# GpSimd's weight sums in other slots, resident blocks filled later, queries loaded in the second layers: a linear-attention and GELU kernel on one core

## The chip, the core and the metric

The kernel runs on one core of one Trainium2 chip. TensorE (PE) multiplies, VectorE (DVE), ScalarE (ACT) and GpSimd (POOL) work on tiles in SBUF and in PSUM, and SyncE (SP) issues the DMAs, one after the other from one queue. The metric is the time of one execution in microseconds (us) of device time; of several runs the median counts. Beside the runs there is one profiled execution with its trace.

## The reference

Linear attention, an RMS norm per head, and a feed-forward network with a GELU, all in fp32:

```python
kv  = einsum('bhsd,bhse->bhde', k, v)            # b=8, h=8, s=576, d=64
o   = einsum('bhsd,bhde->bhse', q, kv)
o   = o / sqrt(mean(o*o, axis=-1) + 1e-6) * g_norm
x   = o.transpose(0, 2, 1, 3).reshape(4608, 512)
h   = x @ w_in                                   # 512 x 2048
y   = (0.5 * h * (1 + erf(h / sqrt(2)))) @ w_out # 2048 x 512
```

## The kernel before

**Arithmetic.** Each operand of the two layers is split into a high part that TensorE's fp32r format holds exactly and a low part, the rest. A product is then three matmuls: high by high, high by low, low by high. The low parts are subtractions on VectorE: `low_x` (L351) and `low_block` (L376) for x, `rest` (L708) for the activations, `low_sums` (L454) and the second half of `split_out` (L1050) for sums of weights. The high parts are copies on ScalarE (`split_out`'s is L1049).

**Chunks.** The 4608 tokens are nine chunks of 512. In chunks 0 and 1 both layers are plain: a chunk has 16 *slots*, and slot i computes one 128-wide block of h (`layer1`, L689, 12 matmuls of 512 columns), its GELU on ScalarE, and what the block before adds to the output (`layer2`, L716, 12 matmuls of 512 columns). Chunk 2 has a plain second layer, but its first layer goes in eight *pairs* of blocks, each by a product form of the Winograd kind with seven products of half size in place of eight (`layer1_pair`, `product` at L554, 12 or 6 matmuls of 256 columns each; L570 copies the first product out of PSUM and L545 adds the rest). In chunks 3 to 8 both layers have this form: the first layer goes in parts (`first_part`, `second_part`, numbered j = 0 to 7, the second part of j following the first part of j + 1), the second layer in 28 *ticks* of 12 matmuls of 256 columns (L1247). `FAST` is 3, `PLAIN` is 2, `NCH` is 9.

**Sums of weights.** The seven-product form wants sums of weight blocks. Those of w_in are made on VectorE in chunk 1 (`sum_weights`: whole blocks at L427, half sums at L438, low parts at L454; `HALVES` tells how many in which slot). Those of w_out are made in eight groups j = 0 to 7: `sum_out(j)` on GpSimd puts together two whole blocks (two additions of 128x512) and makes four sums of 128x256 (all L545); `split_out(j)` then makes the high and low parts, and `send` issues the DMAs that put the products into DRAM. Group 0 is made in slots 12 and 13 of chunk 0, group 1 from slot 15 of chunk 0, groups 2, 3 and 4 in slots 4, 6 and 13 of chunk 1, groups 5, 6 and 7 in pairs of chunk 2. The first addition of each `sum_out` waits for the last GELU that was issued ahead of it, by a dependence written by hand, so that it doesn't start sooner.

**Fetches.** The products of weights lie in DRAM as blocks of 512 KB. `fetch` (L505) brings them into a ring of six SBUF slots, in the order of their use; `used` issues the next fetch as soon as a slot's last reader is issued. Nine blocks of the second layer and some of the first stay resident in SBUF. The pieces of the resident blocks that need no sum are copied from the weights in SBUF by `raw_out(j)` through `product_out` (L411, a DMA from SBUF to SBUF, three of 256 KB for each j).

**Other transfers.** The same SP queue carries the queries of the next chunk but one (`Attn.load`, L222, two loads of 512 KB for a chunk), K and V (`load_kv` L151 and L168, `load_main` L123, `load_tails` L138) and the output (L755 to L758). In the fast chunks the attention of chunk c + 1 is computed during chunk c: its projection and squares in the first layer (`within_layer1`; the fold of the squares is L293), its operands for the first layer in the second (`within_layer2`).

Tile names: `w_in_…`, `w_out_…`, `x_…` and `s_…` are places in SBUF that are reused for many things; only the number behind the name tells one use from the next. `products_in_…` and `products_out_…` are the blocks in DRAM.

Of the kernel before, what the change touches and what calls it, by code (L numbers as in the profile page):

```python
# [8 lines left out]
F32 = mybir.dt.float32  # L9
# [3 lines left out]
ALU = mybir.AluOpType  # L13
# [10 lines left out]
FAST = 3  # L24
# [13 lines left out]
def linear_attn_rms_gelu_ffn(  # L38
# [24 lines left out]
    NF = w_in.shape[0]  # L63
    NCH = NT // CH
# [33 lines left out]
    SPARE = ["s0", "s1", "s2"]  # L98
# [9 lines left out]
        block_tile(name, F32)  # L108


    kv_in, late = {}, {}

    def late_tile(name):

# [88 lines left out]
    class Attn:  # L203
# [144 lines left out]

        def low_x(self, p, eng):
            hi, lo = (self.x[p][:, z].rearrange("p (a n) -> p a n", a=2) for z in range(2))  # L350
            eng.tensor_tensor(out=lo, in0=self.pair(p), in1=hi.bitcast(F32), op=ALU.subtract)  # L351

        def add_blocks(self, k, eng=nc.vector):
            to, a, op, b = {
# [30 lines left out]
    NJ2 = NF // 2  # L385
# [144 lines left out]
    free = []  # L530
# [230 lines left out]
    attn = [Attn(c) for c in range(NCH)]  # L761
    first, second = attn[:2]
# [44 lines left out]
    for d in range(0, 2 * D, BLK):  # L807
        h = d // D * D
        nc.gpsimd.tensor_tensor(
            out=fold[:, d:d + BLK], in0=ident[:, h:h + BLK], in1=ident[:, h + BLK:h + 2 * BLK],  # L810
# [181 lines left out]
    def raw_out(j):  # L992

        t = [parts["out", 2 * j + n].rearrange("p (a n) -> p a n", a=2) for n in range(2)]
        product_out(place_out(j, 0), t[0][:, :, :HALF])
        product_out(place_out(j, 4), t[1][:, :, :HALF])
        product_out(place_out(j, 3), t[1][:, :, HALF:])
# [8 lines left out]
    RAW = [x for j in range(4) for x in ((raw_in, j + 1), (raw_out, j))]  # L1006
    RAW += [(raw_in, 0), (raw_out, 4), (raw_in, 5), (raw_out, 5), (raw_in, 6), (raw_in, 7)]

    wide, sent, latest = {}, [], {}

    def sum_out(j, places=()):

        eng = nc.gpsimd
        if places:
            name = of = None
            whole, s = (block_tile(n, F32)[:, :2 * DM] for n in places)
        else:
            (name, whole), (of, s) = take(), take()
        for n in range(2):
            w = parts["out", 2 * j + n].bitcast(F32)  # L1020
            op = add(whole[:, n * DM:(n + 1) * DM], w[:, HI], w[:, LO], eng=eng)
            if n == 0:
                tc.add_manual_dep(
                    op.ins, latest["gelu"].ins.name,
                    mybir.DependencyInfo(
                        mybir.DependencyClass.Sync, mybir.DependencyReason.DATA
                    ),
                )
        a11, a21, a12, a22 = (whole[:, n * HALF:(n + 1) * HALF] for n in range(4))
        s1, s2, s3, s4 = (s[:, n * HALF:(n + 1) * HALF] for n in range(4))  # L1030
        for o, x, op, y in (
            (s1, a21, ALU.add, a22), (s2, s1, ALU.subtract, a11),
            (s3, a11, ALU.subtract, a21), (s4, a12, ALU.subtract, s2),
        ):
            add(o, x, y, op, eng)
        if name:
            free.append(name)
        wide[j] = of, s
# [41 lines left out]
        for n in {9: (0, 1), 14: (2, 3), 15: (4, 5)}.get(i, ()):  # L1080
            fetch(n)

    EARLY = (0, 0, 4, 6, 13)
    SQUARES = (2, 3, 5, 6)
    HALVES = {1: 2, 2: 2, 3: 2, 4: 1, 5: 1, 7: 2, 8: 1, 9: 1, 10: 1, 11: 2, 12: 1}
    order = list(range(3, len(weights)))

    last = [2]
# [32 lines left out]
    for s in range(PLAIN * NF):  # L1121
        c, i = divmod(s, NF)
        h[s] = layer1(attn[c], i)
        if i == 1 and c:
            store(acc.pop(c - 1), (c - 1) * CH, both=False)
        if c and i in (1, 4):
            place_kv(c + 1, (0, 1) if i == 1 else (2, 3))
        if c == 0:
            g[s] = gelu(h.pop(s))
            if s == 1:  # L1130
                sum_kv(1, (2, 3), kv_ps[1, 0])

            def between():
                if i == 0:
                    for p in (2, 3):
                        attn[0].low_x(p, nc.vector)
                if i in (9, 10):
                    high_w(i - 9)
                    low_w(i - 9)
                if i == 10:  # L1140
                    load_w(len(weights) - 1)
                if i == 1:
                    place_kv(1, range(NP))
                spread_work(c, i)

            convert(i, lambda: g.update({s: rest(*g[s])}), between)
            if s:
                second_layer(s - 1)
            spread_matmuls(c, i)
            if i in (7, 8):  # L1150
                load_kv(c + 2, i - 7)
            if i == 8:
                attn[c + 2].load(0)
            for _ in range(2):
                if i > 6 and RAW:
                    store_raw, j = RAW.pop(0)
                    store_raw(j)
            if i == 12:
                sum_out(0, SPARE[:2])
            if i == 13:  # L1160
                split_out(0, (SPARE[2], SPARE[0]))
                send()
            if i == 15:
                sum_out(1, (SPARE[1], SPARE[0]))
        else:
            spread_matmuls(c, i)
            g[s] = gelu(h.pop(s))
            nxt, k = attn[c + 1], SQUARES.index(i) if i in SQUARES else None
            if k is not None:
                sq = nxt.square(BLOCKS[k])  # L1170
            if i == 12:
                for p in (2, 3):
                    load_kv(c + 2, p)
            sum_weights(i, HALVES.get(i, 0), lambda: g.update({s: rest(*g[s])}))
            if k is not None:
                nxt.reduce(BLOCKS[k], sq)
            if i and i in EARLY:
                sum_out(EARLY.index(i), ("w_in9", SPARE[0]) if i == 13 else ("w_in2", "w_in3"))
            elif i - 1 in EARLY:
                n = max(1, EARLY.index(i - 1))  # L1180
                split_out(n, (SPARE[2:0:-1], ("w_in4", "w_in5"), ("w_in6", "w_in7"),
                              SPARE[1:])[n - 1])
            spread_work(c, i)
            second_layer(s - 1)
            later(c, i)
# [155 lines left out]
    def within_layer1(c, j, second):  # L1341


        nxt = attn[c + 1] if c + 1 < NCH else None
        aft = attn[c + 2] if c + 2 < NCH else None
        at = j, second
        if nxt:
            if second and j < 2 and c == FAST:
                nxt.project(j, [bank(f"a{half}") for half in range(2)])
                for half in range(2):  # L1350
                    nxt.squares((j, half))
            if not second and j < 2 and c > FAST:
                if j == 0:
                    for k, name in enumerate(("acc2", "acc3", "a0", "a1")):
                        nxt.ps[k // 2, k % 2] = bank(name)
                    for p in range(NP):
                        nxt.project_pair(p)
                for half in range(2):
                    nxt.squares((j, half))
            if at == (2, True):  # L1360
                nxt.inv = nxt.rsqrt(nxt.fold(bank("a0")))
            if at in SCALES:
                nxt.scale(SCALES.index(at), nc.gpsimd)
            for k in {(6, False): ("T3", "T1"), (5, True): ("T2", "T4")}.get(at, ()):
                nxt.add_blocks(k, nc.gpsimd)
        if second and c + 2 < B:
            late = int(c == FAST)
            if j - late in (2, 3):
                names["kv", j - late], t = take()
                load_main(c + 2, j - late, t)  # L1370
            if j - late == 3:
                load_tails(c + 2)
            if j - late == 5:
                kv_ps[c + 2, 0] = bank("a1")
                sum_kv(c + 2, range(NP), kv_ps[c + 2, 0])
                free.extend(names.pop(n) for n in (("kv", 2), ("kv", 3), "tails"))
                place_kv(c + 2, range(NP))
        if second and aft and j in (1, 2):
            aft.load(j - 1)

    def next_piece(c, n, eng):
        nxt = attn[c + 1]
        name, t = take(F32R)
# [3 lines left out]

    def within_layer2(c, layer, i):

        if c + 3 < B and i in (8, 18):  # L1390
            load_kv(c + 3, i // 18)
        if c + 1 < NCH:
            step = len(layer.ticks) // 8
            if i % step == step - 1 and i // step < NPR:
                n = i // step
                next_piece(c, n, nc.vector)

    free += ["x4", "x5", "x0", "x1", "w_in12"] + SPARE
    SUMS = {1: (5,), 3: (6,), 5: (7,)}
    SPLITS = {2: (5,), 6: (6,), 7: (7,)}  # L1400
    STEPS = ((3, 1), (3, 2), (4, 0), (4, 2))
    for c in range(PLAIN, FAST):
        for j in range(NJ2):
# [31 lines left out]
    for c in range(FAST, NCH):  # L1435
# [3 lines left out]
        for j, second in parts_of_layer1():  # L1439
# [7 lines left out]
                    send()  # L1447
            else:
                second_part(at, j, blocks)
            if c == FAST and second and j in (2, 5):  # L1450
                raw_out(NJ2 - 2 + j // 3)
                free.extend(f"w_out{n + 2 * (j // 3)}" for n in (NF - 4, NF - 3))
            if j < NJ2 - 1:
                within_layer1(c, j, second)
            if (j, second) == (NJ2 - 1, False):
# [70 lines left out]
```

## Time and profile before

| | before |
|---|---|
| median of 3 runs (lowest to highest) | 787.66 us (785.92 to 788.44) |
| the profiled execution's own time | 787.64 us |
| its span from the first to the last instruction | 785.8 us |
| PE busy | 777.2 us (99%), 6460 matmuls |
| DVE, ACT, POOL busy | 573.6, 352.1, 163.5 us |
| DMA | 239.10 MB, mean 304 GB/s; SP's queue takes 84.8% of 16 engines' span |
| granted TensorE clock | 1.000 of full speed |

Busy time is what an engine spends in instructions; PE's ends are modelled. A row of the list of waits names the engine and tile that waited, what released it, the total in us, the count and the longest. A row of the chain or the timeline gives a start in us from the span's beginning, a duration, an engine, a line and an operation; the timeline also gives the tile written and those read, how many instructions it took together, and in square brackets the idle time before it with what ended it.

### The profile page before, as it was taken

How to read it: one execution, taken by the hardware profiler on the slowest of the kernel's cores; microseconds unless marked ns; L12 is line 12 of the kernel's file. 1: busy time of each engine (PE TensorE's matmuls, PEld its weight loads, DVE VectorE, ACT ScalarE, POOL GpSimd, SP SyncE). 2: the span in 40 equal slices, each digit the busy share in tenths (PEclk: the TensorE clock that was granted, in tenths of full speed). 3: DMA queues.
4: the chain of work that ended last, by engine and by line, in shares of the span. 5: the costliest groups of instructions: out<-in, count | busy, mean ns of one | idle time of the engine just before them, and what ended most of it. 6: DMA issues, size and time to landing. Idle time of an engine off the chain costs nothing.

```text
span 785.8 us, 16444 instructions
## 1 busy us (share of the span) xinstructions
PE 777.2 (99%) x6460; PEld 726.7 (92%) x6460; DVE 573.6 (73%) x1035; ACT 352.1 (45%) x667; POOL 163.5 (21%) x142
## 2 busy tenths in 40 slices
PE   9999999999999999999999999999999999999998
PEld 7888878888899989899999999999999999999998
DVE  3998886798657773769477947795689668965783
ACT  3777545434452332437243624362536343632461
POOL 1000160421223210450027001800171017101200
PEclk9999999999999999999999999999999999999999
DMA  9997966666796789997999798979997989799974
GB/s 347 407 396 255 332 208 241 208 233 241 282 360 220 259 268 370 362 375 284 351 355 362 273 366 319 381 256 319 312 364 257 319 305 323 256 316 340 334 250 168
DMA packets 88368, 239.10 MB, mean 304 GB/s; under 512 B 8804, under 2 KB 29796, under 8 KB 88292
## 3 DMA queue, kind: packets, MB, share of 16 engines
q1 hardware_dynamic: 88288, 238.06, 84.8%
q8 instruction: 51, 0.84, 0.4%
q14 instruction: 25, 0.20, 0.1%
q10 hardware_dynamic: 4, 0.00, 0.0%
HBM read 199.23 MB, written 34.08 MB: 297 GB/s over the span
## 4 chain that ended last, share of the span: by engine, by line
PE 93%; DMA 3%; DVE 2%; issue 1%; ACT 0%; SPq 0%; DVEq 0%; ACTq 0%
PE acc L1247 21%; PE acc L554 18%; PE acc L716 16%; PE h L554 15%; PE h L689 10%; PE a L1247 8%; PE a L188 2%; PE a L241 1%; DMA kv_main<-kv_main 1%; DMA w_in<-products_in 1%; DMA w_in<-qT 1%; PE acc L241 1%; PE h L679 0%; DVE x L351 0%; DVE x L376 0%
## 5 line engine op out<-in xcount | busy, mean ns | idle before, releaser
L716 PE MATMUL acc<-w_out,gh 128*128 128x512 f32 x312 | 97.1, 392 | 0.0
L689 PE MATMUL h<-x,w_in 128*128 128x512 f32 x360 | 87.4, 391 | 0.6 <-DVE x L351 0.6
L689 PEld LDWEIGHTS h<-x,w_in 128*128 128x128 f32 x360 | 67.3, 188 | 15.6 <-DVE x L351 1.3
L716 PEld LDWEIGHTS acc<-w_out,gh 128*128 128x128 f32 x312 | 57.7, 188 | 12.2 <-ACT s L1049 0.2
L702 ACT ACTIVATE gh<-h 128x512 fp32r<-128x512 f32 x39 | 23.3, 597 | 92.5 <-PE h L689 62.4
L716 PE MATMUL acc<-w_out,gl 128*128 128x512 f32 x156 | 60.7, 389 | 0.0
L554 PE MATMUL h<-w_in,w_in 128*128 128x256 f32 x402 | 51.9, 277 | 2.4 <-DMA w_in<-products_in 1.3
L554 PEld LDWEIGHTS h<-w_in,w_in 128*128 128x128 f32 x402 | 48.5, 188 | 2.8 <-ACT w_in L610 1.5
L1247 PE MATMUL acc<-w_in,w_out 128*128 128x256 f32 x408 | 50.6, 276 | 0.0
L554 PE MATMUL acc<-x,w_in 128*128 128x256 f32 x360 | 50.0, 279 | 0.0
L1247 PEld LDWEIGHTS acc<-w_in,w_out 128*128 128x128 f32 x408 | 48.3, 188 | 0.0
L554 PEld LDWEIGHTS acc<-x,w_in 128*128 128x128 f32 x360 | 45.0, 188 | 0.9 <-issue 0.8
L1247 PE MATMUL acc<-w_in,w_in 128*128 128x256 f32 x348 | 43.7, 277 | 0.0
L554 PE MATMUL h<-x,w_in 128*128 128x256 f32 x312 | 42.6, 280 | 0.1
L1247 PE MATMUL acc<-w_in,x 128*128 128x256 f32 x336 | 41.5, 277 | 0.0
L1247 PEld LDWEIGHTS acc<-w_in,w_in 128*128 128x128 f32 x348 | 41.5, 188 | 0.0
L554 PEld LDWEIGHTS h<-x,w_in 128*128 128x128 f32 x312 | 39.6, 189 | 1.4 <-issue 0.7
L1247 PEld LDWEIGHTS acc<-w_in,x 128*128 128x128 f32 x336 | 39.7, 188 | 0.0
L545 DVE TENSOR_TENSOR gl<-acc,gh 128x256 f32<-128x256 f32 (+1 forms) x66 | 29.3, 444 | 13.4 <-ACT gh L591 9.4
L554 PE MATMUL acc<-w_in,w_in 128*128 128x256 f32 x270 | 38.7, 279 | 0.0
L591 ACT COPY gh<-h 128x256 f32<-128x256 f32 x18 | 6.7, 373 | 68.0 <-PE h L554 68.0
L554 PE MATMUL acc<-w_out,w_in 128*128 128x256 f32 x270 | 36.7, 278 | 0.0
(324 smaller groups left out, 1811.8 us busy)
## 6 DMA issues: line engine op xcount, KB each, us to landing
w_in<-products_in SPq DMA_DIRECT2D x172, 512.0 KB, 5.5
w_in<-products_out SPq DMA_DIRECT2D x114, 512.0 KB, 4.9
products_in<-w_in SPq DMA_DIRECT2D x40, 256.0 KB, 3.3
w_in<-w_in SPq DMA_DIRECT2D x16, 512.0 KB, 10.2
kv_main<-kv_main SPq DMA_DIRECT2D x16, 512.0 KB, 6.5
w_out<-w_out SPq DMA_DIRECT2D x16, 512.0 KB, 10.2
q<-qT SPq DMA_DIRECT2D x15, 512.0 KB, 6.9
out<-w SPq DMA_DIRECT2D x17, 256.0 KB, 3.9
```

The costliest lines, as they stand in the source:

```text
L188: nc.tensor.matmul(out=ps[r, n * D:(n + 1) * D], lhsT=k[:, r], rhs=v[:, r], start=(j == 0), stop=(j == NJ),)
L241: nc.tensor.matmul(out=ps[rows(h), p % 2 * HALF + a:p % 2 * HALF + e], lhsT=kv[b % 2][rows(half), p, h ^ half], rhs=q[rows(half), h, a:e], ...
L545: return eng.tensor_tensor(out=out, in0=x, in1=y, op=op)
L554: nc.tensor.matmul(out=out, lhsT=y, rhs=x[:, z, kb], start=first and kb + i == 0, stop=kb == 1 and i == 2, skip_group_check=True,)
L591: nc.scalar.copy(out=u[:, left], in_=a[:, left])
L689: nc.tensor.matmul(out=h, lhsT=parts["in", i][:, w][:, p * P:(p + 1) * P], rhs=at.x[p][:, x], start=(m + p == 0), stop=(m == 2 and p == NP ...
L702: nc.scalar.activation(out=gh, in_=h, func=AF.Gelu)
L716: nc.tensor.matmul(out=ps, lhsT=x[:, ts], rhs=parts["out", i][:, w], start=(i == 0 and m == 0), stop=(m == 2 and (i == NF - 1 or (i, t) == ...
L1247: nc.tensor.matmul(out=self.bank[name][a][:, a * HALF:(a + 1) * HALF], lhsT=x[:, at], rhs=y, start=(k in (0, 2, 1) and n + p + m == 0 and ...
```

## The change

Four things move. No matmul is added, taken away or reordered, and GpSimd's instructions keep their order.

1. *The end of chunk 0.* `sum_out(1)` in slot 15 of chunk 0 waits by its hand-written dependence for the last `low_x` on VectorE, no longer for the last GELU on ScalarE (`behind="x"`). Its `split_out(1)` goes from slot 1 of chunk 1 to slot 2, and `HALVES` moves one combination of w_in's half sums from slot 2 to slot 1.
2. *Chunk 2.* `sum_out` of groups 5, 6 and 7 goes from pairs 1, 3 and 5 to pairs 0, 1 and 3; `split_out(5)` goes from pair 2 to pair 1 (6 and 7 stay at pairs 6 and 7).
3. *Chunk 3, resident blocks.* `raw_out(6)` and `raw_out(7)` go from the second parts 2 and 5 to the second parts 6 and 7, and with them the release of the places w_out12 to w_out15.
4. *Query loads.* The two loads for chunk c + 2 go from the second parts 1 and 2 of chunk c's first layer to ticks 3 and 13 of its second layer, in chunks 3 to 6.

The diff, cut:

```diff
         def low_x(self, p, eng):
...
-            eng.tensor_tensor(out=lo, in0=self.pair(p), in1=hi.bitcast(F32), op=ALU.subtract)
+            latest["x"] = eng.tensor_tensor(out=lo, in0=self.pair(p), in1=hi.bitcast(F32), op=ALU.subtract)
...
-    def sum_out(j, places=()):
+    def sum_out(j, places=(), behind="gelu"):
...
-                    op.ins, latest["gelu"].ins.name,
+                    op.ins, latest[behind].ins.name,
...
-    EARLY = (0, 0, 4, 6, 13)
+    EARLY = {4: 2, 6: 3, 13: 4}
+    SPLIT_AT = {2: (1, ("s2", "s1")), 5: (2, ("w_in4", "w_in5")), 7: (3, ("w_in6", "w_in7")),
+                14: (4, ("s1", "s2"))}
...
-    HALVES = {1: 2, 2: 2, 3: 2, 4: 1, 5: 1, 7: 2, 8: 1, 9: 1, 10: 1, 11: 2, 12: 1}
+    HALVES = {1: 3, 2: 1, 3: 2, 4: 1, 5: 1, 7: 2, 8: 1, 9: 1, 10: 1, 11: 2, 12: 1}
...
             if i == 15:
-                sum_out(1, (SPARE[1], SPARE[0]))
+                sum_out(1, (SPARE[1], SPARE[0]), "x")
...
-        if second and aft and j in (1, 2):
-            aft.load(j - 1)
...
     def within_layer2(c, layer, i):
 
+        if c + 2 < NCH and i in (3, 13):
+            attn[c + 2].load(i // 13)
...
-    SUMS = {1: (5,), 3: (6,), 5: (7,)}
-    SPLITS = {2: (5,), 6: (6,), 7: (7,)}
+    SUMS = {0: (5,), 1: (6,), 3: (7,)}
+    SPLITS = {1: (5,), 6: (6,), 7: (7,)}
...
-            if c == FAST and second and j in (2, 5):
-                raw_out(NJ2 - 2 + j // 3)
-                free.extend(f"w_out{n + 2 * (j // 3)}" for n in (NF - 4, NF - 3))
+            if c == FAST and second and j > 5:
+                raw_out(j)
+                free.extend(f"w_out{2 * j + n}" for n in range(2))
```

SP's queue in the middle of chunk 3's first layer, before. L505 are fetches of weight products, L411 the pieces of a resident block, L222 the query loads, each row one DMA in the order of issue:

```order
L222 DMA q<-qT 128x1024
L505 DMA w_in_1978<-products_in_0_1193 128x1024
L505 DMA w_in_1980<-products_in_1_1197 128x1024
L505 DMA w_in_1545<-products_in_2_1083 128x1024
L411 DMA w_in_3547<-w_out_1045 128x2x256
L411 DMA w_in_3549<-w_out_1107 128x2x256
L411 DMA w_in_3551<-w_out_1107 128x2x256
L222 DMA q<-qT 128x1024
L505 DMA w_in_1610<-products_in_0_1252 128x1024
L505 DMA w_in_2316<-products_in_1_1256 128x1024
```

The same fetches after the change:

```order
L505 DMA w_in_1978<-products_in_0_1193 128x1024
L505 DMA w_in_1980<-products_in_1_1197 128x1024
L505 DMA w_in_1534<-products_in_2_1083 128x1024
L505 DMA w_in_1610<-products_in_0_1252 128x1024
L505 DMA w_in_2316<-products_in_1_1256 128x1024
```

Both query loads and the three pieces are gone from between them. SP's queue at the end of that first layer and the beginning of the second, after; the fetches of `products_out` are the second layer's:

```order
L505 DMA w_in_1534<-products_out_0_890 128x1024
L411 DMA w_in_3832<-w_out_1045 128x2x256
L411 DMA w_in_3834<-w_out_1107 128x2x256
L411 DMA w_in_3836<-w_out_1107 128x2x256
L505 DMA w_in_1610<-products_out_1_1024 128x1024
L411 DMA w_in_3832<-w_out_1227 128x2x256
L411 DMA w_in_3834<-w_out_1333 128x2x256
L411 DMA w_in_3836<-w_out_1333 128x2x256
L505 DMA w_in_2316<-products_out_2_1148 128x1024
L505 DMA w_in_2318<-products_out_0_1274 128x1024
L505 DMA w_in_1978<-products_out_1_1767 128x1024
L222 DMA q<-qT 128x1024
```

Here all six pieces now stand, and the first query load follows three fetches later. VectorE in pairs 1 and 2 of chunk 2, before; L708 are the low parts of the activations, L283 the sums of squares of the next chunk, L570 and L545 read pair 2's products from PSUM (`h`), L1050 are the low parts of group 5:

```order
L708 TENSOR_TENSOR w_in_2499<-h_2425,w_in_2499 128x512
L283 TENSOR_REDUCE part<-sq 128x16 x2
L570 COPY w_in_2322<-h_2567 128x256
L545 TENSOR_TENSOR w_in_2322<-h_2567,w_in_2322 128x256
L545 TENSOR_TENSOR w_in_2322<-h_2568,w_in_2322 128x256
L545 TENSOR_TENSOR h_2567<-h_2567,w_in_2322 128x256
L545 TENSOR_TENSOR w_in_2322<-h_2568,w_in_2322 128x256
L545 TENSOR_TENSOR h_2568<-h_2568,w_in_2322 128x256 x2
L708 TENSOR_TENSOR gl<-h_2567,gh 128x512
L708 TENSOR_TENSOR gl<-h_2568,gh 128x512
L1050 TENSOR_TENSOR w_in_2635<-x_2504,w_in_2635 128x2x256
L1050 TENSOR_TENSOR s_2638<-x_2504,s_2638 128x2x256
```

And after:

```order
L708 TENSOR_TENSOR w_in_2507<-h_2433,w_in_2507 128x512
L1050 TENSOR_TENSOR x_2511<-x_2385,x_2511 128x2x256
L1050 TENSOR_TENSOR w_in_2514<-x_2385,w_in_2514 128x2x256
L283 TENSOR_REDUCE part<-sq 128x16 x2
L570 COPY w_in_2322<-h_2581 128x256
L545 TENSOR_TENSOR w_in_2322<-h_2581,w_in_2322 128x256
```

The two low parts of group 5 now stand ahead of the reductions and of the copy that opens pair 2's additions, no longer behind pair 2's activations.

More of the change, by code (lines that the diff above doesn't have):

```diff
@@ L108, in linear_attn_rms_gelu_ffn @@
         block_tile(name, F32)
-    kv_in, late = {}, {}
+    kv_in, late, latest = {}, {}, {}
     def late_tile(name):
@@ L1007, in linear_attn_rms_gelu_ffn @@
     RAW += [(raw_in, 0), (raw_out, 4), (raw_in, 5), (raw_out, 5), (raw_in, 6), (raw_in, 7)]
-    wide, sent, latest = {}, [], {}
-    def sum_out(j, places=()):
+    wide, sent = {}, []
+    def sum_out(j, places=(), behind="gelu"):
         eng = nc.gpsimd
@@ L1176, in linear_attn_rms_gelu_ffn @@
                 nxt.reduce(BLOCKS[k], sq)
[L1177 to L1182, printed above, removed]
+            if i in EARLY:
+                sum_out(EARLY[i], ("w_in9", SPARE[0]) if i == 13 else ("w_in2", "w_in3"))
+            elif i in SPLIT_AT:
+                split_out(*SPLIT_AT[i])
             spread_work(c, i)
```

## The prediction

> **What bounds the kernel now.** First the page's busy times, for the engine that sets the end; then the list of waits of that engine; then the chain that ended last, stage by stage, to price each wait with what it drags behind it.
>
> ```profile
> span 785.8 us, 16444 instructions
> PE 777.2 (99%) x6460; PEld 726.7 (92%) x6460; DVE 573.6 (73%) x1035; ACT 352.1 (45%) x667; POOL 163.5 (21%) x142
> ```
>
> TensorE is busy 99% of the span. This change neither adds nor removes a matmul, so all that it can win is idle time of TensorE and matmuls that run slower than their neighbours; all it can lose is a new wait there. The profiled execution took 787.64 us, 1.8 us more than its span, and the median of the three runs shown is 787.66, so I work from 787.64. Their spread, 785.92 to 788.44, is why I call anything within 0.3% (2.4 us) no change.
>
> ```profile
> PE h L554 <- DMA w_in<-products_in: 1.3, 1, 1.3
> PE h L554 <- DVE w_in L545: 1.1, 1, 1.1
> PE h L689 <- DVE x L351: 0.6, 1, 0.6
> ```
>
> Columns: total us, times, longest. These three, once each, are TensorE's only long waits after the start-up. They lie at 331.9, 276.1 and 114.8 us, and each stands beside something this change moves.
>
> **Part a: GpSimd's sum at the end of chunk 0 (wait 0.6).**
>
> ```profile
> 106.55 2.88 PE L689 MATMUL h<-x,w_in 128*128 128x512 f32 x12
> 109.27 0.61 PE L716 MATMUL acc<-w_out,gh 128*128 128x512 f32 x2
> ...
> 111.99 2.81 PE L689 MATMUL h<-x,w_in 128*128 128x512 f32 x11
> ...
> 115.88 0.69 PE L188 MATMUL a<-kv_main 112*64 112x64 f32 x16
> ```
>
> Twelve such matmuls normally take 109.27 - 106.55 = 2.72; here 115.88 - 111.99 = 3.89. That is 1.17 lost, more than the 0.6 in the wait list, since the matmuls around a wait lose time too. I count 1.1, as a little goes to the switch to the small matmuls behind it, which stays.
>
> ```profile
> 112.47 2.92 DVE L351 TENSOR_TENSOR x<-o,x 128x512 fp32r<-128x512 f32 x2
> 110.70 3.00 POOL L545 TENSOR_TENSOR s<-w_out 128x512 f32<-128x512 f32 x2 [3.20 <-ACT h L703]
> 284.60 0.68 DVE L376 TENSOR_TENSOR x<-z,x 128x512 fp32r<-128x512 f32 x1
> ```
>
> Late are the last two low parts of x. They take 2.92 for two while GpSimd sums weights from 110.70; the same kind of subtraction with GpSimd idle takes 0.68 (last row). The new dependence lets the sum start only behind the second of them. Then they end by 112.47 + 2 x 0.68 = 113.8, and TensorE first wants one at its tenth matmul, 111.99 + 9 x 0.227 = 114.0. The wait goes: -1.1. Lowest value: 0.6, the bare wait; highest 1.17. Behind the waiting instruction on GpSimd stands only the rest of this sum: it ends some 3 us later, at about 119, and is read in slot 2 of chunk 1, after 130. That the copies move from slot 1 to slot 2, and one combination of half weights from 2 to 1, exchanges four 128x512 steps on VectorE there against the two copies; the subtraction for the slot's own activations slips by about 1 us and is read a slot (5.4 us: 2 x 2.72) later. Cost 0; if that cover failed, about 1 us, once.
>
> **Part b: chunk 2's sums (wait 1.1).**
>
> ```profile
> 273.15 1.59 PE L554 MATMUL h<-x,w_in 128*128 128x256 f32 x12
> 279.42 5.65 PE L716 MATMUL acc<-w_out,w_in 128*128 128x512 f32 x24
> 284.90 1.59 PE L554 MATMUL h<-x,w_in 128*128 128x256 f32 x12
> 289.74 0.63 PE L716 MATMUL acc<-w_out,gh 128*128 128x512 f32 x2
> ...
> 271.07 1.28 DVE L366 TENSOR_TENSOR z<-o,w 128x512 f32<-128x512 f32 x1
> 275.12 1.22 DVE L376 TENSOR_TENSOR x<-o,x 128x512 fp32r<-128x512 f32 x1
> 270.50 3.00 POOL L545 TENSOR_TENSOR x<-w_out 128x512 f32<-128x512 f32 x2 [17.00 <-ACT h L703]
> ```
>
> A pair of blocks in the first layer takes 289.74 - 284.90 = 4.84; the pair at 273.15 takes 6.27, so 1.43 is lost. VectorE's four operations from 271.07 end at 276.34 under the sum that GpSimd began at 270.50; at 0.68 each they end near 273.8, before the copy that TensorE waits for can start at all (1.64 into the pair in the clean case). The sum of rows 14 and 15 moves from pair 5 to pair 3, where today's sum 6 runs, and 6 moves to today's place of 5. So -1.43 (lowest 1.1, the bare wait). The only new place is sum 5 at pair 0, and its copies move to pair 1, beside sum 6:
>
> ```profile
> 225.06 2.53 POOL L545 TENSOR_TENSOR x<-w_out 128x512 f32<-128x512 f32 x2 [23.65 <-ACT h L703]
> 229.87 0.74 POOL L545 TENSOR_TENSOR x<-x,x 128x256 f32<-128x256 f32 x1
> 227.00 0.71 DVE L283 TRANSPOSE_TENSOR_REDUCE part<-sq 128x16 f32<-128x512 f32 x1 [1.30 <-ACT sq L273]
> 230.65 0.42 DVE L570 COPY w_in<-h 128x256 f32<-128x256 f32 x1 [1.56 <-PE h L554]
> 231.11 0.42 DVE L545 TENSOR_TENSOR w_in<-h,w_in 128x256 f32<-128x256 f32 x1
> 230.45 3.56 PE L554 MATMUL h<-w_in,w_in 128*128 128x256 f32 x30
> ```
>
> A sum lasts 5.5 us and ends before the next pair. At pair 1 VectorE gets two copies more, from 225.7. At 1.2 to 1.5 each (rows above) they end at 228.1 to 228.7. The two reductions with ScalarE's square between them took 227.00 to 229.09 (230.65 less its idle 1.56), so now they end at 230.2 to 230.8, against a copy due at 230.65. TensorE needs the add behind that copy at 230.45 + 12 x 0.113 = 231.8, and it ends at 231.53: 0.27 to spare. Cost 0; upper end 0.4.
>
> The Trainium skill's page "SBUF — State Buffer", section "Who interferes with whom", says that a VectorE operation with two SBUF inputs and a GpSimd operation that reads SBUF take turns at one port for whole instructions. By it parts a and b win as said, but it speaks against the copies at pair 1: each would wait out one 1.27 us add, they would end near 229.0, and TensorE would lose about 0.2; the time would be 782.8 instead of 782.6.
>
> **Part c: the first layers of chunks 3 to 6 (wait 1.3).**
>
> ```profile
> 320.65 0.17 PE a L293 x2
> ...
> 324.61 8.51 DMA w_in<-products_in
> ...
> 346.90 3.15 PE acc L1247 x27
> ...
> 404.31 0.17 PE a L293 x2
> ...
> 414.12 2.84 PE h L554 x24
> ...
> 428.62 1.44 PE acc L1247 x12
> ...
> 495.83 0.12 issue
> 495.95 2.96 PE h L554 x24
> ...
> 656.50 2.72 PE h L554 x24
> ```
>
> These are from the chain. From the fold (L293) to the second layer (L1247) the same instructions take 26.25 in chunk 3 and 24.31 in chunk 4. Chunk 4 itself has 24 matmuls at 2.84 that take 2.72 in chunk 7: matmuls whose weights land just in time run slow. So chunk 3 loses 26.25 - 24.31 + 0.12 = 2.06, chunk 4 0.12, chunk 5 0.24 + 0.12 = 0.36; chunk 6 shows nothing of the kind, and I count 0.
>
> ```profile
> 303.00:347.00 44.00, 42.63 (x432) 40.71 (x431) 28.29 (x57) 17.40 (x34) 19.46 (x14) 1.00 0.99 368
> 347.00:385.00 38.00, 38.00 (x337) 38.00 (x336) 29.15 (x49) 19.27 (x36) 0.00 (x0) 1.00 0.87 319
> 428.50:466.70 38.20, 38.20 (x339) 38.20 (x338) 29.50 (x50) 19.38 (x36) 0.00 (x0) 1.00 0.88 311
> ...
> DMA to landing us min/median/max: 4.5/7.5/9.7
> DMA to landing us min/median/max: 4.4/5.9/6.5
> ```
>
> The last two columns of the stage rows are DMA share and GB/s; the landing lines are the fetches of L505 in chunk 3's first and second layer. In the first layer the queue is full (0.99). A fetch goes out when its slot of six is free and is wanted 72 matmuls, 8.3 us, later; landings reach 9.7. At 368 GB/s a query load (512 KB) is 1.42 us of queue, a resident piece (256 KB) 0.71. Two and three of these go away ahead of the late fetch: 2 x 1.42 + 3 x 0.71 = 5.0 us, against a wait of 1.3. What is late next is nothing by these rows: the fetch has 3.6 us to spare. -2.06 - 0.12 - 0.36 = -2.54; lowest 1.3, the bare wait.
>
> What comes back: in the second layers a fetch is wanted at least seven steps of twelve matmuls, 9.6 us, after it goes out. Landings reach 6.5, so even 1.42 for a query load leaves 1.7, and the two loads stand ten steps (13.7 us) apart. Of 38 us, 0.12 (4.6 us) of the queue is free, and two loads take 2.8. The six resident pieces now go out at the end of the first layer and are wanted at the sixth step, 6.8 us into the second; in a queue with 5 us less in it they land in about 5. The loads they delay are wanted 12 us later. SP waits for nothing new: the query buffers were read at the start of the first layer. The late release of w_out12 to w_out15 gives operands other slots; their earlier readers are done. Cost 0; upper end 1.5, the size of today's wait, if the pieces came late.
>
> **Sum.** -1.1 - 1.43 - 2.54 = -5.07: 787.64 - 5.07 = 782.57, say 782.6. With all lowest values and both new costs: 0.6 + 1.1 + 1.3 - 0.4 - 1.5 = 1.1 gained, 786.5; with all highest, 1.17 + 1.43 + 2.54 = 5.14, 782.5.
>
> **Rivals.**
> - *The second layers choke* (the other side). Query loads in the second layers of chunks 3 to 6 make a fetch later than its 9.6 us. For: 0.87 to 0.88 of the queue is taken there already. Against: the 1.7 us left above. It needs 3.1 us on the longest landing, two loads in one burst. At chunk 3's price, 2.06 each: 787.64 - 5.07 + 4 x 2.06 = 790.8. It decides from 1.3 us per layer on. Chance 0.05.
> - *The fetch wait stays*, since the K and V loads crowd the same queue: only a and b win, 787.64 - 2.53 = 785.1. For: they too stand there. Against: chunk 4 has them and two query loads, and no wait. 0.12.
> - *A wait changes place*: a resident piece at the sixth step, or VectorE at pair 1, gives 1 to 2 us back, 783.6 to 784.6. 0.12.
> - *It does nothing measurable*: TensorE, freed from these waits, meets the next late thing a few us on; 785.3 to 787.6. For: VectorE is at 73%. Against: VectorE idles before most matmul groups. 0.08.
> - The forecast, 782.6: 0.63, its own range 781.3 to 783.6, the sum plus the scatter of a median.
>
> Faster by over 0.3% takes the forecast, the changed place, and about half of the second rival: 0.81. Within 0.3%: 0.14. Slower: 0.05. The range that leaves out 2 in 10 runs from 780.9 to 785.8.
>
> **What would show it.** The three waits are gone from TensorE's list; L351's two take 1.3 at the end of chunk 0, L366 and L376 0.68 in pair 5; GpSimd's sums start near 113, 216, 225 and 247; fold to second layer takes about 24.2 in chunk 3; longest landings of L505 under 8.3 in first layers, near 8 in second. Wrong it would be if TensorE waits in a second layer, or at 353 for a resident piece, or at pair 2 for VectorE.

## The result and the profile after

| | before | after |
|---|---|---|
| median | 788.05 us (785.92 to 788.53, 4 runs) | 782.52 us (782.34 to 782.59, 4 runs) |
| the profiled execution | 787.64, span 785.8 | 782.55, span 780.8 |

The ratio of after to before is 0.9933, 95% interval 0.9919 to 0.9947: the change is worth 4.2 to 6.4 us. The two profiled executions, which the prediction's sum was made against, differ by 5.09. A second set of five runs of the changed kernel gave 782.48 (782.17 to 783.23), ratio 0.9927. Beside the medians the spread has changed: the four runs of before lie 2.6 us apart, those of after 0.25.

The page's head and TensorE's part of the list of waits, after:

```profile
span 780.8 us, 16442 instructions
PE 774.7 (99%) x6460; PEld 725.0 (93%) x6460; DVE 570.2 (73%) x1035; ACT 352.1 (45%) x667; POOL 161.8 (21%) x142
```

```profile
PE h L796 <- DVE w_in L765: 1.1, 1, 1.1
PE a L188 <- DMA w_out<-kv_main: 0.8, 2, 0.5
PE h L679 <- DVE w_out L657: 0.5, 1, 0.5
PE h L842 <- ACT gl L831: 0.4, 1, 0.4
PE acc L241 <- ACT kv L199: 0.3, 1, 0.3
```

These five all lie in the start-up, ahead of 30 us. The three waits behind it that the prediction named (1.3 for a fetch, 1.1 for L545, 0.6 for L351) are gone, and no other has come. TensorE's own busy time fell too, from 777.2 to 774.7, with the same 6460 matmuls: those around a wait counted as longer, and so did the 24 in chunk 4 whose weights came just in time (2.84 before, 2.72 now, below).

**The end of chunk 0**, timeline of the three engines, after:

```profile
111.91 2.88 PE L689 MATMUL h<-x,w_in 128*128 128x512 f32 x12
114.72 0.69 PE L188 MATMUL a<-kv_main 112*64 112x64 f32 x16
111.78 1.28 DVE L351 TENSOR_TENSOR x<-o,x 128x512 fp32r<-128x512 f32 x2
113.21 2.52 POOL L545 TENSOR_TENSOR s<-w_out 128x512 f32<-128x512 f32 x2 [5.79 <-DVE x L351]
```

The two low parts take 1.28 where they took 2.92, GpSimd starts only behind them, and from the slot's first matmul to the next group 2.81 pass in place of 3.89: 1.08 won.

**Chunk 2**, pair 5 and then pair 1, after:

```profile
272.00 1.59 PE L554 MATMUL h<-x,w_in 128*128 128x256 f32 x12
276.83 5.63 PE L716 MATMUL acc<-w_out,w_in 128*128 128x512 f32 x24
269.91 0.68 DVE L366 TENSOR_TENSOR z<-o,w 128x512 f32<-128x512 f32 x1
271.72 0.69 DVE L376 TENSOR_TENSOR w_out<-o,w_out 128x512 fp32r<-128x512 f32 x1
273.63 0.42 DVE L570 COPY w_in<-h 128x256 f32<-128x256 f32 x1 [1.23 <-PE h L554]
...
227.86 1.60 PE L554 MATMUL h<-x,w_in 128*128 128x256 f32 x12
224.47 1.26 DVE L1050 TENSOR_TENSOR x<-x,x 128x512 fp32r<-128x512 f32 x1
225.66 1.78 DVE L1050 TENSOR_TENSOR w_in<-x,w_in 128x512 fp32r<-128x512 f32 x1
228.72 0.71 DVE L283 TRANSPOSE_TENSOR_REDUCE part<-sq 128x16 f32<-128x512 f32 x1 [0.66 <-ACT sq L273]
229.50 0.42 DVE L570 COPY w_in<-h 128x256 f32<-128x256 f32 x1
```

In pair 5 VectorE is done at 272.41, and its copy (L570) now waits for TensorE, as in the clean pairs: 276.83 - 272.00 = 4.83 for the pair in place of 6.27. At pair 1 the two copies that came in take 1.26 and 1.78 beside sum 6, the reductions end at 229.43, and pair 2's copy goes out at 229.50. That is 1.64 after its pair's start at 227.86, the same as in a clean pair: VectorE was in time by 0.07, and nothing was lost.

**Chunk 3**, the chain from the fold to the second layer with one row of chunk 4 behind it, and the landings of L505's fetches in that first layer and the second layer behind it, after:

```profile
318.05 0.17 PE a L293 x2
...
342.37 21.85 PE acc L1247 x192
...
409.60 2.72 PE h L554 x24
```

```profile
DMA to landing us min/median/max: 3.5/5.6/8.8
...
DMA to landing us min/median/max: 3.3/6.1/7.0
```

The stretch takes 24.32 (it took 26.25), and the 24 matmuls of chunk 4, the last row of the chain, take 2.72 (they took 2.84). The longest landing in the first layer fell from 9.7 to 8.8 and the median is 5.6; in the second layer the longest rose from 6.5 to 7.0. The queue in the two stages:

```profile
300.50:342.40 41.90, 41.90 (x431) 40.34 (x430) 28.90 (x58) 18.27 (x36) 19.61 (x14) 1.00 0.95 345
342.40:380.50 38.10, 38.10 (x337) 38.10 (x336) 28.98 (x49) 18.50 (x34) 0.00 (x0) 1.00 0.97 369
```

Of the layers of the fast chunks the fullest (DMA share, last column but one) is now chunk 3's second, with 0.97, and TensorE is busy through all of it.

### The profile page after: what moved, and what is told of

Same layout as the page of the kernel before. It is cut to its first block, busy times and chain, and to the rows that moved or that the text cites. A ratio compares the mean times of both kernels' runs of the same rounds, so it can differ in the third digit from the quotient of the medians.

```text
span 780.8 us, 16442 instructions
## 1 busy us (share of the span) xinstructions
PE 774.7 (99%) x6460; PEld 725.0 (93%) x6460; DVE 570.2 (73%) x1035; ACT 352.1 (45%) x667; POOL 161.8 (21%) x142
## 4 chain that ended last, share of the span: by engine, by line
PE 97%; DMA 1%; DVE 1%; issue 0%; ACT 0%; DVEq 0%
PE acc L1247 21%; PE acc L554 19%; PE acc L716 17%; PE h L554 16%; PE h L689 11%; PE a L1247 8%; PE a L188 2%; PE a L241 1%; DMA w_out<-kv_main 1%; PE acc L241 1%; PE h L679 0%; PE h L842 0%; DVE w_out L657 0%; DVE o L912 0%; PE a L293 0%
## 5 line engine op out<-in xcount | busy, mean ns | idle before, releaser
L1247 PE MATMUL acc<-w_in,w_out 128*128 128x256 f32 x444 | 54.9, 276 | 0.0
L1247 PEld LDWEIGHTS acc<-w_in,w_out 128*128 128x128 f32 x444 | 52.5, 188 | 0.0
L554 PE MATMUL acc<-w_out,w_in 128*128 128x256 f32 x330 | 46.4, 279 | 0.0
L554 PE MATMUL h<-w_in,w_in 128*128 128x256 f32 x366 | 46.3, 276 | 0.0
L554 PEld LDWEIGHTS h<-w_in,w_in 128*128 128x128 f32 x366 | 43.8, 188 | 0.0
L554 PEld LDWEIGHTS acc<-w_out,w_in 128*128 128x128 f32 x330 | 41.4, 188 | 0.3 <-issue 0.2
L1247 PE MATMUL acc<-w_in,x 128*128 128x256 f32 x312 | 39.0, 276 | 0.0
L545 DVE TENSOR_TENSOR gl<-acc,gh 128x256 f32<-128x256 f32 (+1 forms) x66 | 29.2, 443 | 13.2 <-ACT gh L591 9.4
L1247 PEld LDWEIGHTS acc<-w_in,x 128*128 128x128 f32 x312 | 37.1, 188 | 0.0
L708 DVE TENSOR_TENSOR gl<-h,gh 128x512 fp32r<-128x512 f32 x39 | 26.8, 686 | 14.0 <-ACT h L703 13.8
L1247 PE MATMUL acc<-w_in,w_in 128*128 128x256 f32 x288 | 36.2, 277 | 0.0
```

Of the source, the lines that this page charges most:

```text
L545: return eng.tensor_tensor(out=out, in0=x, in1=y, op=op)
L554: nc.tensor.matmul(out=out, lhsT=y, rhs=x[:, z, kb], start=first and kb + i == 0, stop=kb == 1 and i == 2, skip_group_check=True,)
L708: nc.vector.tensor_tensor(out=gl, in0=h, in1=gh.bitcast(F32), op=ALU.subtract)
L1247: nc.tensor.matmul(out=self.bank[name][a][:, a * HALF:(a + 1) * HALF], lhsT=x[:, at], rhs=y, start=(k in (0, 2, 1) and n + p + m == 0 and ...
```

## The experiments

The kernels ran in four sets, each on one chip and in turn with the kernel before; the sets are the first section's four, the next three sections' four, the three of the bytes, and the last one alone. The ratio is always to the kernel before of the same set.

### The parts one by one

Four kernels: the kernel before with one part of the diff each. For a, the lines on `latest`, `behind`, `SPLIT_AT` and `HALVES`; for b:

```diff
-    SUMS = {1: (5,), 3: (6,), 5: (7,)}
-    SPLITS = {2: (5,), 6: (6,), 7: (7,)}
+    SUMS = {0: (5,), 1: (6,), 3: (7,)}
+    SPLITS = {1: (5,), 6: (6,), 7: (7,)}
```

and part c in its two halves, `aft.load` into `within_layer2`, and `raw_out` with its releases to the second parts 6 and 7.

> The kernel before with part a alone (the sum at the end of chunk 0 behind the last low part of x). My theory, GpSimd's sum slows VectorE's subtractions beside it: TensorE's wait for L351 goes and the time falls by 1.1 us against the kernel before, to a ratio near 0.9986; the two subtractions take 1.3 us in place of 2.92. Rival, VectorE is late there for its own queue: the wait stays at 0.6 us, the ratio is 1.000. The waits for the fetch and for L545 stay as they are by both.

> The kernel before with part b alone (chunk 2's sums in pairs 0, 1 and 3). My theory: pair 5 loses its 1.1 us wait and 1.43 us in all, no other pair gets slower, ratio near 0.9982. Rival, the contention goes to pair 1, where two copies and a sum now meet: 0.2 to 0.4 us come back and pair 2 takes 5.0 to 5.2 us in place of 4.84; ratio 0.9987.

> The kernel before with the query loads alone moved to the second layers. The late fetch of chunk 3 has 2 x 1.42 = 2.8 us less ahead of it, which is more than its wait of 1.3: my theory gives all of part c, 2.5 us (chunk 3's 2.06, and 0.48 in chunks 4 and 5, which only the queries touch), ratio 0.9968. Rival, the resident pieces are what holds the fetch up: about 0.5 us, ratio 0.9994, and the wait stays at about 1. The spread of the runs should shrink if the fetch's wait is what scatters from run to run.

> The kernel before with the resident pieces alone moved to the end of chunk 3's first layer. 3 x 0.71 = 2.1 us go from ahead of the late fetch, more than its wait of 1.3. My theory, what counts is the sum of bytes ahead: chunk 3 wins 1.7 to 2.06 us by this alone too, chunks 4 and 5 nothing, ratio 0.9974 to 0.9978, so that the two moves of part c together are far less than their sum. Rival, each move carries its own share and they add up: about 1 us here, ratio 0.9987, with 0.3 to 0.6 us of the wait left.

| part alone | median | lowest to highest | ratio, 95% interval |
|---|---|---|---|
| a | 786.78 | 785.29 to 788.81 (12 runs) | 0.9986 (0.9975 to 0.9997) |
| b | 786.47 | 784.92 to 787.86 (12) | 0.9981 (0.9968 to 0.9993) |
| c, queries | 785.19 | 784.73 to 785.78 (7) | 0.9965 (0.9953 to 0.9978) |
| c, pieces | 786.08 | 785.32 to 787.53 (12) | 0.9976 (0.9967 to 0.9986) |
| the kernel before | 787.79 | 786.28 to 790.61 (30) | 1 |

In us of 787.8 the ratios are 1.1, 1.5, 2.8 and 1.9. All four together would be 7.3; a, b and the whole of c (which the change has) are 5.3 by the first ratio, so that c as a whole, which was not run alone, gives 5.3 - 1.1 - 1.5 = 2.7. By these medians the two halves of c are not additive: the queries alone give about all of it, the pieces alone two thirds. Each interval is 0.8 to 1.0 us to a side, so the shares are rough.

In the lists of waits each of a and b takes away its own wait and leaves the other's: a-only has no wait for L351 (its two subtractions take 1.29) and still the 1.1 for L545, b-only has no wait for L545 (pair 5 takes 4.83) and still the 0.6 for L351.

For part c the lists say less. Rows of the a-only, the b-only, the queries-only and the pieces-only kernel:

```profile
PE h L554 <- DMA w_in<-products_in: 2.9, 3, 1.0
```

```profile
PE acc L554 <- DMA w_in<-products_in: 0.4, 2, 0.2
```

```profile
PE acc L554 <- DMA w_in<-products_in: 0.5, 1, 0.5
```

```profile
PE h L554 <- DMA w_in<-products_in: 0.4, 1, 0.4
```

The first is the surprise of this study. Part a touches no fetch, and in this execution there were three waits of about 1 us, in chunks 3, 4 and 5 (at 329, 413 and 496 us), where the profiled execution of before had 1.34, none and 0.12. The order of the fetches in these chunks is the same in both kernels, so I read the difference as one between executions: this one took 788.81, the slowest of its kernel's twelve, whose own runs differ by 3.5 us. The b-only kernel, with the same fetches too, had only two waits of 0.2, in chunk 3. So one profile can't tell how much each half of c shrinks the waits; the medians above have to. Neither half alone removes the waits in its profile: with the queries moved 0.5 is left in chunk 3 (at 335 us), where the pieces still stand, with the pieces moved 0.4 in chunk 4, where the queries still stand. The expectation of the queries' whole 2.06 in chunk 3 was thus too clean, though the sum came out. The spread did shrink, to 1.05 us over 7 runs with the queries moved, as against 3.5 over 12 for a alone.

### One sum back in its old pair

The changed kernel with group 7's sum back in pair 5:

```diff
-    SUMS = {0: (5,), 1: (6,), 3: (7,)}
+    SUMS = {0: (5,), 1: (6,), 5: (7,)}
```

> The changed kernel with the sum of group 7 put back from pair 3 to pair 5, everything else changed. My theory, it is this one sum that slows VectorE's four operations ahead of pair 5's copy: the wait for L545 comes back with 1.1 us, 1.43 us in all, so 783.9 to 784.0 in place of 782.5, ratio to the kernel before near 0.9951. Rival, VectorE was late in pair 5 because it carried group 5's copies and reductions from the pairs ahead, and these are gone: no wait, 782.5, ratio 0.9933.

783.96 us (783.64 to 784.11, 5 runs), ratio 0.9951 (0.9939 to 0.9963): 1.48 over the changed kernel's 782.48 (two other variants of it in the same set, in the section after next, took 782.62 and 782.54), with the wait back to the last digit:

```profile
PE h L554 <- DVE w_in L545: 1.1, 1, 1.1
```

```profile
269.74 1.29 DVE L366 TENSOR_TENSOR z<-o,w 128x512 f32<-128x512 f32 x1
270.94 2.93 DVE L376 TENSOR_TENSOR x<-o,x 128x512 fp32r<-128x512 f32 x2
269.17 3.00 POOL L545 TENSOR_TENSOR x<-w_out 128x512 f32<-128x512 f32 x2 [39.09 <-ACT h L703]
```

The work that VectorE carries in the pairs ahead is the changed kernel's here, so it is the one sum beside them that makes these operations late. The rival is out.

### How the two engines get in each other's way

The kernel before, with the two large additions of every sum cut by columns:

```diff
-            op = add(whole[:, n * DM:(n + 1) * DM], w[:, HI], w[:, LO], eng=eng)
-            if n == 0:
+            to, hi, lo = whole[:, n * DM:(n + 1) * DM], w[:, HI], w[:, LO]
+            for m in range(4):
+                at = slice(m * P, (m + 1) * P)
+                op = add(to[:, at], hi[:, at], lo[:, at], eng=eng)
+                if n + m == 0:
...
```

> The kernel before with GpSimd's two additions of 128x512 in each sum cut into four of 128x128 each, at the same places. It tells how GpSimd and VectorE get in each other's way. If they take turns by whole instructions, VectorE waits a quarter as long for each: the two L351 beside the sum take 1.9 to 2.1 us in place of 2.92, the first operations of pair 5 about 0.95 each in place of 1.28 to 1.78, the two waits shrink from 0.6 and 1.1 us to under 0.3 each, and the time falls by 1.5 to 2.3 us, ratio 0.997 to 0.998. If they share a bandwidth, VectorE's operations stay as slow as they are for as long as the sum lasts, 2.9 us for the two L351, and the ratio is 1.000.

785.51 us (784.75 to 787.5, 12 runs), ratio 0.9976 (0.9967 to 0.9985). Chunk 0's end and pair 5 in this kernel:

```profile
112.85 1.81 DVE L351 TENSOR_TENSOR x<-o,x 128x512 fp32r<-128x512 f32 x2
111.49 4.73 POOL L545 TENSOR_TENSOR s<-w_out 128x128 f32<-128x128 f32 x8 [2.93 <-ACT h L703]
270.79 0.87 DVE L366 TENSOR_TENSOR z<-o,w 128x512 f32<-128x512 f32 x1
271.58 0.95 DVE L376 TENSOR_TENSOR x<-o,x 128x512 fp32r<-128x512 f32 x1
274.51 0.42 DVE L570 COPY w_in<-h 128x256 f32<-128x256 f32 x1 [0.24 <-PE h L554]
```

The sums run beside the same work of VectorE as before, but in pair 5 its operations take 0.87 to 0.95 in place of 1.22 to 1.78, the two L351 take 1.81 in place of 2.92, and both waits of TensorE are gone from the list; two for a fetch, 1.7 in all, are left. A shared bandwidth should have left them slow for as long as the sum lasts. This alone is not quite enough against it, since the additions cut in four also ask for less in a given time (4.73 us for the eight in place of 3.00 for the two). That the engines take turns by whole instructions is shown directly by the rows of two single additions at pair 1 of the changed kernel, beside the two copies shown above:

```profile
223.91 1.28 POOL L545 TENSOR_TENSOR s<-w_out 128x512 f32<-128x512 f32 x1 [3.23 <-ACT h L703]
225.14 1.75 POOL L545 TENSOR_TENSOR s<-w_out 128x512 f32<-128x512 f32 x1
```

The additions end at 225.19 and 226.89; VectorE's copies (1.26 from 224.47, 1.78 from 225.66) end at 225.73 and 227.44, each some 0.55 behind an addition's end, and the second addition, which spans the first copy's end, takes 1.75 in place of 1.28. The Trainium skill's page "SBUF — State Buffer", section "Who interferes with whom", says this (an exclusive lock for the whole instruction, when VectorE has two inputs in SBUF and GpSimd reads SBUF), and the runs agree with it.

### A fuller queue in the second layers

The changed kernel with both query loads at tick 3, and the changed kernel with two further transfers in each second layer:

```diff
-        if c + 2 < NCH and i in (3, 13):
-            attn[c + 2].load(i // 13)
+        if c + 2 < NCH and i == 3:
+            for n in range(2):
+                attn[c + 2].load(n)
```

```diff
+        if c + 2 < NCH and i in (4, 14):
+            if "extra" not in products:
+                products["extra"] = dram.tile([P, 2 * DM], F32, name="extra")
+            nc.sync.dma_start(out=products["extra"], in_=qT[c + 2, i // 14])
```

> The changed kernel with both query loads at tick 3 of the second layer, in place of ticks 3 and 13. The longest landing of a fetch there (7.0 us in chunk 3 after the change) grows by one load, 1.42, to 8.4, still under the 9.6 us at which it is wanted. My theory: no wait, 782.5 within 0.3, ratio 0.9933. Rival, the prediction's choke: a fetch comes late in each of four second layers, up to 2.06 us each, 784 to 790.

> The changed kernel with two more transfers of 512 KB in each second layer of chunks 3 to 6, at ticks 4 and 14, from the queries to a place in DRAM that nobody reads; the output is the same. They ask for 2 x 1.42 = 2.8 us more of a queue that is busy for 0.97 of 38 us in chunk 3 and 0.94 in chunk 4, so in chunk 3 the backlog ends 1.7 us longer than now. My theory: that still fits into the slack of 2.6 us (9.6 less 7.0) in the second layers, and what is late shows at the start of the next first layer: 782.5 to 784.5, ratio 0.9933 to 0.996. Rival, the choke: waits at L1247 or L554 in all of chunks 3 to 6, 2 us each, 790, ratio above 1.002.

782.62 us (782.2 to 783.23), ratio 0.9936 (0.9923 to 0.9948), and 782.54 us (782.24 to 783.3), ratio 0.9934 (0.992 to 0.9947), five runs each: neither costs anything. The longest landings of L505 in the second layers of chunks 3 and 4 were 8.1 and 7.9 us with the burst, where 8.4 was expected. With the further transfers:

```profile
DMA to landing us min/median/max: 5.6/6.9/8.1
DMA to landing us min/median/max: 4.3/7.9/9.8
```

With the further transfers chunk 3's second layer has a full queue:

```profile
342.00:380.50 38.50, 38.50 (x341) 38.50 (x340) 29.34 (x49) 18.61 (x35) 0.47 (x1) 1.00 1.01 383
```

In chunk 4 the fetch that went out at 452.65 took 9.8 us. It landed at 462.46, just as TensorE came to it at the start of chunk 5, and some 0.3 us are lost there (0.10 idle, and 24 matmuls at 3.02 in place of 2.78). The choke that the prediction feared thus stands off by about these 2.8 us of transfers in a layer, and not by much more.

### Bytes or issues in the first layers

What of the query loads made the fetches late: their bytes, a wait for their buffers, or SP's time to issue them? Their buffers it was not: in the kernel before SP's list of waits has no row for L222 from 300 to 700 us. For the other two, at the two old places (second parts 1 and 2 of the first layers of chunks 3 to 6) the changed kernel got transfers from DRAM to DRAM that nobody reads, once of 512 KB and once four of 4 KB each:

```diff
+        if second and aft and j in (1, 2):
...
+            nc.sync.dma_start(out=products["extra"], in_=qT[c + 2, j - 1])
```

```diff
+        if second and aft and j in (1, 2):
...
+            for n in range(4):
+                m = 4 * (j - 1) + n
+                nc.sync.dma_start(out=products["extra"][m:m + 1], in_=qT[c + 2, j - 1, m:m + 1])
```

> The changed kernel with two transfers of 512 KB put where the query loads stood (second parts 1 and 2 of the first layers of chunks 3 to 6), from the queries to a place in DRAM that nobody reads; the true query loads stay in the second layers, so the output is the same. Theory, the bytes ahead of a fetch make it late: what the pieces-alone kernel still lost to the query loads comes back, 0.5 to 1.1 us, 783.0 to 783.6, with waits for a fetch of 0.1 to 1 us in one or two of chunks 3 to 5, landings above 9 us, and a spread of the runs above 1 us. Rival, the query loads held SP's queue up because their buffers came free late: these transfers wait for no buffer, so the time stays at 782.5 and landings at 8 to 9 us.

> The changed kernel itself, as the measure for its neighbours: 782.3 to 782.7, spread under 0.6 us, ratio 0.9933.

> The changed kernel with four DMAs of 4 KB at each of the two places in the first layers of chunks 3 to 6 where the query loads stood, eight for each layer; nobody reads what they write. They bring no bytes to speak of, but SP needs 0.3 us for each issue (about 1.3 us for four), and each holds one of the eight DMA semaphores until it lands. Theory, bytes make fetches late: 782.5, no wait for a fetch. Rival, what counts is the number of DMAs ahead of a fetch, by SP's issue time or by the semaphores: fetches go out 1.3 us later at each place and as many land late as with the query loads, 783.0 to 784.5.

| | median | lowest to highest (5 runs) | ratio, 95% interval |
|---|---|---|---|
| two of 512 KB | 783.89 | 782.80 to 785.55 | 0.9944 (0.9929 to 0.9960) |
| the changed kernel | 782.48 | 782.17 to 783.23 | 0.9927 (0.9915 to 0.9940) |
| eight of 4 KB | 782.66 | 782.40 to 783.18 | 0.9928 (0.9914 to 0.9942) |

The two of 512 KB bring 1.4 us back in the median, somewhat more than the 0.5 to 1.1 expected, and the spread: 2.75 us. (The changed kernel's own five runs spread over 1.06, where under 0.6 was expected, and the intervals of the two ratios overlap.) The list of waits of the kernel with 512 KB:

```profile
PE h L554 <- DMA w_in<-products_in: 1.0, 2, 0.5
```

They lie in chunks 4 and 5 (at 409 and 492 us). But these transfers brought more than their bytes. Both of a layer write the same place, and SP held the second back until the first had landed, so they did wait, against the expectation. SP's list of waits in chunks 3 to 6, and the chain into the wait of chunk 5 (L1381 is the added transfer):

```profile
SPq L1381 <- DMA extra<-qT: 6.9, 4, 2.1
```

```profile
477.13 7.34 DMA extra<-qT
...
484.55 0.51 SPq L1381
...
485.48 6.90 DMA w_in<-products_in
```

The late fetch stood behind the second transfer and went out 1.6 us after its slot had come free. So this kernel doesn't tell bytes from a held queue.

The eight small DMAs kept SP busy longer than the query loads had. Their issue in chunk 3 of this kernel, and that of the two query loads in chunk 3 of the kernel before (ns, least, median and most of one):

```profile
L1383 SPq DMA_DIRECT2D extra<-qT x8: 495/584/588, 311.7 to 319.5; - x8
```

```profile
L222 SPq DMA_DIRECT2D q<-qT x2: 423/700/976, 314.3 to 322.4; - x2
```

That is some 4.6 us of SP against 1.4, and yet the median stays within 0.2 us of the changed kernel's, and the list has no wait for a fetch. In this profile some 0.5 us are lost in chunk 4 all the same.

All the profiles together tell more. In chunks 4 and 5 the first fetch behind the fold goes out 1.84 us after the fold's first matmul (L293), when its slot comes free, unless SP is held up; the next one in chunk 3 at 3.20. How late it went out and how long it then took to land, in us:

| kernel, chunk | sent out late by | to landing | TensorE's wait |
|---|---|---|---|
| before, 3 | 0.9 | 8.5 | 1.3 |
| a alone, 3 | 2.0 | 7.1 | 1.0 |
| a alone, 4 and 5 | 0 | 8.9, 9.0 | 0.9, 1.0 |
| pieces alone, 4 | 0 | 8.4 | 0.4 |
| two of 512 KB, 4 and 5 | 1.0, 1.6 | 7.5, 6.9 | 0.5, 0.5 |
| eight of 4 KB, 4 and 5 | 1.5, 2.2 | 6.6, 5.0 | none listed |
| changed, 4 and 5 | 0 | 7.0, 6.1 | none |

TensorE waits when the two together pass about 8.0 us. Bytes lengthen the landing: in chunks 4 and 5 this fetch took 7.6 to 9.0 in the five profiles with the query loads in front of it (before, a, b, pieces alone, cut additions) and 5.8 to 7.0 in the seven with the loads in the second layers and nothing in their place. The number of DMAs does not, by the 6.6 and 5.0 with eight small ones in front, though that fetch went out late. A held SP sends the fetch out late. In chunk 3 of the kernel before both came together, for SP was still issuing the three pieces (2.01 us) and the second load (0.98); the chain of the a-only kernel runs through these issues:

```profile
319.45 0.64 SPq L411
...
321.86 1.40 SPq L222
...
323.36 7.08 DMA w_in<-products_in
```

### The other way to a and b

The kernel before with both halves of c and the additions cut in four, every sum in its old slot:

> The kernel before with part c (queries and pieces moved) and GpSimd's large additions cut in four, but every sum in its old slot (parts a and b not made). If parts a and b bought nothing but VectorE's freedom from GpSimd's long instructions, cutting them buys the same, and this kernel comes to the changed one's time: 782.3 to 782.9, ratio near 0.993, no wait for L351 or L545 and spread under 1 us. If moving the sums did something else besides, it stays behind by up to 2.5 us, 783 to 785.

782.50 us (782.21 to 782.81, 5 runs), ratio 0.9929 (0.9915 to 0.9943), with no wait of TensorE behind the start-up. Shorter instructions at the old places buy what moving the sums buys: the medians are 0.02 us apart, on different chips, and the ratios agree within their intervals. It beats the kernel before but not the changed one.

## Why the prediction was right, point by point

**The sum.** Forecast 787.64 - 5.07 = 782.57, measured 782.52 in the median and 782.55 in the profiled execution. Parts a and b were confirmed alone, c by its halves and by what is left of the whole: a 1.1 forecast, 1.1 by ratio and 1.08 in the timeline; b 1.43, 1.5 and 1.44 (6.27 - 4.83); c 2.54 against 2.7. The intervals of the ratios are 0.8 to 1.0 us to each side, so the sizes within a part rest on the traces.

**Part a.** The cause (GpSimd's sum beside VectorE), the price of a subtraction without it and the lack of a follow-up hold. The sum started at 113.21, forecast near 113, and its later copies cost nothing.

**Part b.** Pair 5 as forecast. At pair 1 the copies took 1.26 and 1.78, the second above the 1.2 to 1.5 that was taken for each; the margin held since the first copy waited only for the rest of an addition. The reckoning by the Trainium skill's rule (782.8) had each copy wait out a whole one; the rule holds, that use of it was too dear by 0.2.

**Part c.** The cause is shown: the transfers in front of the fetches. The prediction counted their bytes alone, and in chunks 4 and 5 that is what the landings show. In chunk 3 it left out a term: a fetch was to go out when its slot is free, but the late one went out 0.9 us after that, held by SP's issues of the pieces and the load. Besides, the step "chunk 3 loses 2.06, chunk 4 0.12, chunk 5 0.36" read one execution as if it were the kernel. The a-only kernel's execution, with the same fetches, waited 0.9 to 1.0 us in each of chunks 3, 4 and 5. The forecast's sum held since the profiled execution stood near the median (787.64 against 788.05); that was luck, since the a-only kernel was profiled at 788.81 with 2.9 us of such waits, and the b-only kernel had hardly any.

**What came back.** Nothing, as forecast, but with other numbers. The six resident pieces of the changed kernel were forecast to land in about 5 us:

```profile
DMA to landing us min/median/max: 6.3/8.0/8.1
```

They took 6.3 to 8.1; the first layer's queue is still 0.95 full. The one that the sixth step wants went out at 342.07 and landed at 348.7, and that step began at 349.1: the margin was about 0.4 us, where the prediction had 1.8 (6.8 less 5). The longest landing in a first layer was to be under 8.3 and was 8.8, in a second layer near 8 and was 7.0. The 8.3 us after which a late fetch was to cost time is about right, 8.0 by the table above. The landing of 8.8 cost nothing because 80 matmuls of attention (2.48 us) come before that fetch is used; the longest landing of a stage need not be the one that TensorE waits for.

**The rivals.** The choke of the second layers is out by two kernels that loaded them further. The fetch wait staying and the wait changing place are out by the list of waits. "Nothing measurable" is out by the ratio, 0.9933 with an interval up to 0.9947.

## What to carry to other kernels

When TensorE is at 99%, look for the single waits in its list, find what runs beside each, and price the wait with the slow matmuls around it: here 0.6 was worth 1.1 and 1.1 was worth 1.4. A wait on another engine may be undone by moving the neighbour or by cutting the neighbour's instructions shorter; both gave the same. Read a wait for a DMA as one draw of many where the queue is full: profile a second execution, or look at the spread of the runs, before its microseconds are assigned to a place. For each late transfer ask two things, when it went out and how long it took; and look whether a transfer put in for a test waits itself, before its effect is put down to its bytes.

## What the runs showed of the hardware beyond expectation

With the same order of fetches, waits in a full queue were 1.3 us in chunk 3 and 0.1 in chunk 5 in one profile (before), 0.9 to 1.0 in each of chunks 3, 4 and 5 in another (a alone), and none above 0.2 in a third (b alone). The runs of every kernel that had such waits in its profile and the query loads or their bytes in the first layers spread over 2.2 us or more (a, b and the pieces alone and the cut additions in 12 runs each, the 512 KB put back in 5); those of every kernel with the queries moved and nothing in their place over 1.1 us or less (4 to 7 runs each). Why one execution's landings are longer than another's is not settled by these runs.

A 128x512 addition on GpSimd cut into four of 128x128 takes 0.46 us each, 1.8 for the four, in place of 1.28, and gives VectorE its turn after 0.46 in place of 1.28.
